# One kilobyte-sized load, two queues: the convolution taps issued by ScalarE instead of SyncE

## The chip, the core and the metric

The kernel runs on one core of a Trainium2 chip. The core has five engines with an instruction queue each: TensorE (PE, matmuls and their weight loads PEld), VectorE (DVE), ScalarE (ACT), GpSimd (POOL) and SyncE (SP, which only issues transfers here). Engines work through their own instructions in order and wait for each other by semaphores. Sixteen DMA engines move data. A queue name with a q at the end (SPq, ACTq, PEq) is an engine's instruction queue: what it shows is issue or waiting, not computing.

The metric is the device time in microseconds (us) of one execution. Before the change it is 263.19 us, the median of three runs (262.81 to 263.39).

## What is computed

One layer of a model on 2048 tokens of width 640: a LayerNorm, a gated long convolution (A), and a gated feed-forward block with 1728 inner columns (B), both with a residual sum. Cut to what matters:

```python
def A(q, k, v, shift_k, ssm_k, ssm_D):           # q is LayerNorm(x)
    k_shift = sum(k_pad[:, t:t+S, :] * shift_k[:, 3-t] for t in range(4))   # 4 taps per channel
    kv = k_shift * v
    y = irfft(rfft(kv, 2*S) * rfft(ssm_k, 2*S))[:S]                         # causal convolution of length S
    return q * (y + kv * ssm_D)

def B(x, w_gate, w_up, w_down):
    return (silu(x @ w_gate) * (x @ w_up)) @ w_down

x = A_q
h  = x + A(layernorm(x), A_k, A_v, A_shift_k, A_ssm_k, A_ssm_D)
h2 = h + B(layernorm(h), B_w_gate, B_w_up, B_w_down)
```

`A_shift_k`, the taps, is a 640 x 4 array in bf16, 5 KB in all.

## The kernel before

The 2048 tokens are cut into four blocks of 512. A block's 512 tokens lie as 128 partitions times four rows. For each block the kernel forms kv (shift convolution of k, times v), transforms kv and the long filter with matrices of cosines and sines held in `WF`, multiplies and sums the spectra on VectorE, transforms back with `WI`, and runs LayerNorm and the feed-forward block. All phases of all blocks are interleaved.

The interleaving is written out by hand. The kernel first makes a list of operations (`plan.add`, with the helpers `pe`, `act`, `dve`, `load`, `evict`), numbered in the order in which the code adds them. `Plan.run` (L147) then goes through the tuple `ORDER` (L43) and emits the operations in that order; a negative entry ~n means operation n with its other engine (a PSUM copy on VectorE instead of ScalarE). Each operation's instructions go to their engine's queue in the order of emission. So the table sets the order within every engine, and the waits between engines follow from who reads and writes what. On-chip buffers come from small pools (four PSUM buffers `ps`, twelve `big`, five `row` and so on) and are handed out in table order, the oldest free one first.

The beginning of the table, which is what the change touches:

```python
ORDER = (
    0, 3, 1, 18, 19, 20, 21, 26, 5, 4, 11, 12, 9, 7, 8, 22, 23, 10, 24, -26, 27, 28, 29, ...
    ... 14, 13, 191, 16, 17, 15, 193, 350, ... 418, 6, 32, 30, 31, 33, 34, 37, 35,
    -37, 38, 41, -43, 118, 39, 40, 65, -67, ... 56, ...
```

The operations with their lines in the profile:

- 0 and 1 (L866, L867): the identity matrix for transposes, made by VectorE and GpSimd.
- 3 and 4 (L471, SyncE): the two halves of block 0 of k. 11, 12, 14 and 13 (L276, L271, L264, L900, SyncE): block 0 of q (`x`), of v and of the filter `ssm_k` (`g`), and `WF`.
- **5 (L875, SyncE): the taps.** The 640 x 4 array is read as five partitions of 1 KB, into the tile `tap5` (`tap` in the profile).
- 18 to 25: the four rows of k are transposed by PE (L484, five matmuls of 128 x 128 each) and copied from PSUM (L486): 19, 21 and 23 by ScalarE, 25 (entry -26) by VectorE.
- 7 (L886): PE turns the taps with four small transposes. 8 (L888): ScalarE copies them to `tapw`. 9 (L892, L893) folds the identity into a small one, and 10 (L895, VectorE) makes `diag`, the taps on small diagonals.
- 27 and 32 (L505): the shift convolution as matmuls of k against `diag`, 112 for four groups of 128 channels, 28 for the fifth. 28 to 31, 33 and 34 (L527, VectorE): the products with v.
- 6 (L880): 24 matmuls of the identity with itself, whose result nobody reads. They keep PE at work between 27 and 32.
- 35 to 42: g is transposed by PE (L392) and copied (L394), rows 0 and 3 by VectorE and 1 and 2 by ScalarE.
- 110 to 117: the first LayerNorm's statistics, two sweeps over each of the four rows of q by ScalarE (L630 the means, L578 the squares).
- 65, 56 and so on (L309): the forward transforms of kv and g, copied from PSUM at L298 (ScalarE) and L301 (VectorE).

In each engine's own queue the start thus reads as follows.

- SyncE: 3, 5, 4, 11, 12, 14, 13, then the transposing loads of the next block of k (L473).
- PE: 18, 20, 7, 22, 24, 27, 6, 32, 37, 35, 41, 39, 65, 56.
- ScalarE: a table load, 19, 21, 8, 23, the eight statistics, 38, 40.
- VectorE: 0, 26, 9, 10, 25, 28 to 31, 33, 34, 36, 42.

Of the kernel before, what the change touches and what calls it, by code (L numbers as in the profile page):

```python
# [19 lines left out]
P = 128  # L20
# [151 lines left out]
def kernel(ctx: ExitStack, tc: tile.TileContext, A_q, A_k, A_v, A_shift_k, A_ssm_k, A_ssm_D, B_x,  # L172
          B_w_gate, B_w_up, B_w_down, out):
    nc = tc.nc
# [20 lines left out]
    def new(kind):  # L195
        return Buf(views.get(kind, (kind,))[0], kind)

    def fixed(shp, dt, name):
        return Buf(None, None, const.tile(shp, dt, name=name))

    def ap(b):
        if b.pool is None:
            return b.ap
        t = place[b.pool][b.at]
        _, how, sizes = views.get(b.kind, (None, None, None))
        return t.rearrange(how, **sizes) if how else t
# [15 lines left out]
    def load(nbytes, fn, w, r=()):  # L222
        return plan.add("sp", nbytes / 300.0, fn, r, w)
# [27 lines left out]
    tap5 = fixed([KT, P * 4], BF16, "tap5")  # L251
# [214 lines left out]
    def load_k(j):  # L466

        kT = new("kT")
        if j == 0 and not K0TURN:
            for lo in (0, 2):  # L470
                load(MB // 2, lambda lo=lo: nc.sync.dma_start(out=plain(kT)[:, lo:lo + 2], in_=block(kk, j)[:, lo:lo + 2, :]), [(kT, ("in", lo // 2))])  # L471
        for r in range(R) if j or K0TURN else ():
            plan.add("turn", MB / 4 / 300.0, lambda r=r: nc.sync.dma_start(  # L473
                out=ap(kT)[:, :, r, PAD:], in_=block(kk, j)[:, r, :], transpose=True), [], [(kT, r)])
        return kT
# [396 lines left out]
            nc.gpsimd.memset(t[64:P, NC_FULL, :], 0.0)  # L872
    plan.add("pool", 2000, blank, [], [blanks])
    k = load_k(0)
    load(1e3, lambda: nc.sync.dma_start(out=ap(tap5), in_=A_shift_k.rearrange("(c p) t -> c (p t)", p=P)), [tap5])  # L875
    idle = new("ps")

    def warm():
# [43 lines left out]
    for j in range(1, NB):  # L922
        plan.block = j
        g = load_g(j)
        if j == 1:
            load(P * NC_FULL * D * 2, lambda: nc.sync.dma_start(
                out=ap(wd)[:, 0:NC_FULL, :], in_=B_w_down[0:NC_FULL * P, :].rearrange("(c p) d -> p c d", p=P)), [(wd, 0)])
# [67 lines left out]
```

## Time and profile before

| | |
|---|---|
| median of three runs | 263.19 us (262.81 to 263.39) |
| the profiled execution's own time | 263.05 us |
| its span, first to last instruction | 261.4 us |
| PE busy in the span | 249.5 us, 95% |
| VectorE busy | 207.8 us, 79% |
| ScalarE busy | 172.9 us, 66% |
| mean granted TensorE clock | 0.999 |
| moved by DMA | 40.82 MB, mean 156 GB/s |

Times in the views are counted from the start of the span. A row of the chain of waits reads: start, length, what. A row of the timeline reads: start, length, engine, line, operation, output <- input, shape, count of merged instructions, and in brackets how long the engine had been idle and what ended it. "x10" rows merge ten instructions; the length is that of the whole row. Matmuls are pipelined, so that the length of one matmul is longer than the distance between two. The landing time of a transfer is counted from its issue.

### The profile page before, as it was taken

Reading aid. Unit: us, or ns where it says so; the run is one execution under the profiler, and the core shown is the slowest. Engines: PE = TensorE matmul, PEld = TensorE weight load, DVE = VectorE, ACT = ScalarE, POOL = GpSimd, SP = SyncE. Lnnn points to the kernel's source line nnn. Section 1 sums busy time; section 2 is a strip of 40 time slices with the busy share of each in tenths; the row PEclk is TensorE's granted clock in tenths of the full one; section 3 lists DMA queues with packets and bytes.
Section 4 is the critical chain, followed back from the end, with each engine's and each line's share of the span. In section 5 each row is a group of like instructions: output and inputs, shape, how many; then the busy total and the mean of one; then the engine's idle time right before and its main releaser. Section 6 shows DMA issues by size and latency. Waiting matters only on the chain.

```text
span 261.4 us, 5121 instructions
## 1 busy us (share of the span) xinstructions
PE 249.5 (95%) x2040; PEld 148.1 (57%) x2040; DVE 207.8 (79%) x325; ACT 172.9 (66%) x294; POOL 18.3 (7%) x26
## 2 busy tenths in 40 slices
PE   3989997999999999999999999999999999999995
PEld 2866674544555677654446667544447764444673
DVE  1579999999999999999999999999999831122132
ACT  4798999999959788757787857154465744434300
POOL 0001000001200013000001300200040121000000
PEclk9999999999999999999999999999999999999999
DMA  6999698998887669579077606796299942000002
GB/s 199 301 235 265 179 174 181 278 261 179 249 277 209 148 127 204 119 223 271 19 212 116 101 0 73 185 286 162 52 319 246 218 50 25 3 0 0 0 15 87
DMA packets 73235, 40.82 MB, mean 156 GB/s; under 512 B 33462, under 2 KB 71164, under 8 KB 73212
## 3 DMA queue, kind: packets, MB, share of 16 engines
q1 hardware_dynamic: 70908, 37.88, 58.2%
q0 software_dynamic: 2304, 2.62, 7.0%
q8 instruction: 16, 0.26, 0.4%
q14 instruction: 7, 0.06, 0.1%
HBM read 30.01 MB, written 4.59 MB: 132 GB/s over the span
## 4 chain that ended last, share of the span: by engine, by line
PE 72%; DVE 14%; ACT 7%; DMA 3%; issue 2%; SPq 0%; ACTq 0%
PE ps L776 32%; PE ps L843 22%; PE ps L309 9%; PE ps L696 4%; PE ps L811 4%; DMA big<-in_A_q_dram 3%; DVE S L539 2%; ACT S L298 2%; DVE S L566 2%; DVE big L565 2%; ACT row L578 2%; DVE big L539 2%; DVE tT L802 1%; ACT row L630 1%; DVE S L437 1%
## 5 line engine op out<-in xcount | busy, mean ns | idle before, releaser
L776 PE MATMUL ps<-big,big 128*128 128x512 bf16 x480 | 105.8, 379 | 0.3 <-ACT sg L820 0.2
L776 PEld LDWEIGHTS <-big 128*128 128x128 bf16 x480 | 46.8, 98 | 56.1 <-issue 1.1
L843 PE MATMUL ps<-wd,tT 128*128 128x320 bf16 x448 | 63.5, 299 | 0.0
L843 PEld LDWEIGHTS <-tT 128*128 128x128 bf16 x448 | 43.7, 98 | 17.4
L793 ACT ACTIVATE sg<-ps 128x1024 bf16<-128x1024 f32 (+1 forms) x28 | 27.0, 965 | 34.7 <-PE ps L776 17.6
L309 PE MATMUL ps<-big,WF 128*128 128x320 bf16 x224 | 35.6, 299 | 1.9 <-ACT big L394 0.8
L566 DVE TENSOR_TENSOR S<-S,big 128x2560 bf16<-128x2560 bf16 x24 | 35.2, 1479 | 0.0
L565 DVE TENSOR_TENSOR big<-S,S 128x2560 bf16<-128x2560 bf16 x24 | 35.2, 1479 | 0.0
L802 DVE TENSOR_TENSOR tT<-sg,sg 128x1024 bf16<-128x1024 bf16 (+1 forms) x26 | 16.7, 642 | 19.4 <-ACT sg L800 19.3
L309 PEld LDWEIGHTS <-WF 128*128 128x128 bf16 x224 | 21.8, 97 | 13.2 <-issue 3.3
L800 ACT CAST sg<-ps 128x1024 bf16<-128x1024 f32 (+1 forms) x26 | 24.6, 947 | 4.9 <-PE ps L776 4.8
L578 ACT ACTIVATE row<-big 128x640 bf16<-128x640 bf16 x32 | 23.6, 742 | 3.7 <-DVE big L714 3.3
L298 ACT CAST S<-ps 128x320 bf16<-128x320 f32 (+1 forms) x36 | 18.0, 547 | 3.8 <-PE ps L309 3.4
L641 ACT ACTIVATE row<-big,sm 128x640 bf16<-128x640 bf16 x18 | 15.8, 916 | 6.0 <-DVE sm L591 6.0
L849 POOL DMA_DIRECT2D out_dram<-row x12 | 10.6, 1022 | 96.5 <-ACT row L848 95.0
L696 PEld LDWEIGHTS <-WI 128*128 128x128 bf16 x128 | 12.4, 98 | 6.0 <-issue 1.1
L696 PE MATMUL ps<-S,WI 128*128 128x320 bf16 x96 | 15.0, 299 | 0.4 <-DVE S L539 0.4
L298 ACT ACTIVATE big<-ps 128x640 bf16<-128x640 f32 (+1 forms) x23 | 13.9, 634 | 2.1 <-PE ps L309 2.0
L811 PE MATMUL ps<-big,big 128*128 128x512 bf16 x60 | 14.3, 379 | 0.0
L708 DVE SCALAR_TENSOR_TENSOR row<-row,ps 128x640 bf16<-128x640 bf16 x16 | 12.8, 813 | 0.2
L630 ACT ACTIVATE row<-big 128x640 bf16<-128x640 bf16 x16 | 11.8, 740 | 1.6 <-DMA big<-in_A_q_dram 1.6
L539 DVE TENSOR_TENSOR big<-S,S 128x2560 bf16<-128x2560 bf16 (+1 forms) x10 | 12.1, 1219 | 0.1
(83 smaller groups left out, 229.2 us busy)
## 6 DMA issues: line engine op xcount, KB each, us to landing
big<-in_B_w_up_dram SPq DMA_DIRECT2D x24, 320.0 KB, 5.1
big<-in_B_w_gate_dram SPq DMA_DIRECT2D x24, 320.0 KB, 5.0
big<-in_A_q_dram SPq DMA_DIRECT2D x4, 640.0 KB, 4.7
big<-in_A_v_dram SPq DMA_DIRECT2D x4, 640.0 KB, 4.3
big<-in_A_ssm_k_dram SPq DMA_DIRECT2D x4, 640.0 KB, 8.2
wd<-in_B_w_down_dram SPq DMA_DIRECT2D x1, 2080.0 KB
out_dram<-big SPq DMA_DIRECT2D x3, 640.0 KB, 5.3
out_dram<-row POOLq DMA_DIRECT2D x12, 160.0 KB, 5.4
```

Source lines behind the costliest of these rows:

```text
L298: (lambda: nc.scalar.activation(dst(), src(), ACT.Copy, scale=2.0)) if twice else (lambda: nc.scalar.copy(dst(), src())),
L309: nc.tensor.matmul(ap(ps)[:, h, 0:NH], w, ap(src)[:, r, h * NH:(h + 1) * NH], start=(first and i == 0), stop=(last and i == len(rs) - 1), ...
L539: return lambda: f(*(x() for x in args))
L565: dve(1490, lambda b=b, xs=xs, hs=hs: nc.vector.tensor_mul(flat2(b), X.part(xs), H.part(hs)), [X.at(xs), H.at(hs)], [b])
L566: dve(1490, lambda b=b, dst=dst, f=f: f(A.part(dst), A.part(dst), flat2(b)), [b], [A.at(dst)])
L578: act(930, lambda r=r, junk=junk: nc.scalar.activation(ap(junk), ap(x)[:, r, :], ACT.Square, scale=D ** -0.5, accum_out=sm(s, 1)[:, r:r + ...
L696: nc.tensor.matmul(ap(ps)[:, w, 0:NH], m, src[:, w * NH:(w + 1) * NH], start=(i == 0), stop=(i == len(terms) - 1))
L776: nc.tensor.matmul(of(ps, i), ap(w)[:, k, off:off + P], ap(hT)[:, k, lo:lo + n], start=(k == 0), stop=(k == KT - 1))
L793: act(1010 if wide else 600, lambda: nc.scalar.activation(of(sg), of(*gate), ACT.Silu), [gate[0]] if gate[0] is up[0] else [(gate[0], gate ...
L800: op = plan.add("act", 1010 if wide else 590, lambda: nc.scalar.copy(of(co), of(*up)), psu + [sg], [co] + tt, ("dve", 1230 if wide else 69 ...
L811: nc.tensor.matmul(ap(ps)[:, i, :], ap(w)[:, k, off:off + P], ap(hT)[:, k, :], start=(k == 0), stop=(k == KT - 1))
L843: nc.tensor.matmul(ap(to)[:, hf, 0:NH], ap(tT)[:, c, at:at + P], ap(wd)[:, c, hf * NH:(hf + 1) * NH], start=(c == order[0]), stop=(c == or ...
```

## The change

One word changes: the load of the taps is started on ScalarE's queue instead of SyncE's.

```diff
     k = load_k(0)
-    load(1e3, lambda: nc.sync.dma_start(out=ap(tap5), in_=A_shift_k.rearrange("(c p) t -> c (p t)", p=P)), [tap5])
+    load(1e3, lambda: nc.scalar.dma_start(out=ap(tap5), in_=A_shift_k.rearrange("(c p) t -> c (p t)", p=P)), [tap5])
     idle = new("ps")
```

The list of operations, their numbers and the order table stay as they are, and operation 5 keeps its place in the table: behind 21 and 26, ahead of 4. SyncE's queue has one issue less, ScalarE's one more. The other transfers stay on SyncE.

## The prediction

> **What bounds the kernel now.** I read the chain of work that ended last first, because a start-up load matters only if the chain passes through it.
>
> ```profile
> 1.28 0.35 SPq L875
> 1.63 0.05 issue
> 1.68 0.35 SPq L471
> ...
> 2.08 6.85 DMA big<-in_A_q_dram
> ...
> 8.95 0.83 ACT row L630 x2
> ...
> 14.82 0.58 ACT big L394
> ...
> 15.45 7.77 PE ps L309 x54
> ```
>
> Columns: start, length, what. The chain begins in SyncE's issues, the taps (L875) among them, goes through the landing of q at 8.93, then through ScalarE's eight LayerNorm statistics (L630, L578) to the copy at L394, which gives back a PSUM buffer; only then does PE begin the long run of transform matmuls at 15.45. So the first 15.45 us are ScalarE's, and ScalarE's start is the landing of q. The next question is whether a shift at 15.45 is swallowed later. The table of stretches (busy PE, PEld, DVE, ACT, POOL in turn) answers it:
>
> ```profile
> 15.45:26.50 11.05, 11.05 (x78) 7.42 (x77) 9.12 (x21) 9.92 (x28) 0.70 (x1) 1.00 1.16 249
> 26.50:54.00 27.50, 25.44 (x299) 16.15 (x299) 26.26 (x55) 27.25 (x46) 0.00 (x0) 1.00 0.91 199
> 54.00:88.00 34.00, 33.66 (x312) 17.84 (x311) 34.00 (x41) 30.20 (x54) 2.75 (x3) 1.00 0.89 240
> 88.00:261.40 173.40, 169.61 (x1145) 98.49 (x1144) 131.74 (x194) 95.67 (x147) 14.11 (x16) 1.00 0.52 118
> ```
>
> In each stretch one engine has almost no idle time: PE 11.05 of 11.05, ACT 27.25 of 27.50, DVE 34.00 of 34.00, PE 169.61 of 173.40. There is no slack in which a late start disappears, so I carry a shift at 15.45 to the end one for one.
>
> The start itself, in order of time (start, length, engine, line, work, and in brackets the idle time before it and what ended it):
>
> ```profile
> 4.07 1.25 PE L484 MATMUL ps<-ident,kT 128*128 128x128 bf16 x10 [4.07 <-DMA kT<-in_A_k_dram]
> 4.82 1.29 ACT L486 COPY kT<-ps 128x640 bf16<-128x640 bf16 x2 [2.72 <-PE ps L484]
> ...
> 5.25 0.29 PE L886 MATMUL ps<-ident,tap 5*128 5x5 bf16 x4
> ...
> 5.94 1.25 PE L484 MATMUL ps<-ident,kT 128*128 128x128 bf16 x10 [0.40 <-DMA kT<-in_A_k_dram]
> 5.99 0.23 ACT L888 COPY tapw<-ps 128x20 bf16<-128x20 bf16 x1
> 6.26 0.82 DVE L895 TENSOR_TENSOR diag<-eye,tapw 128x640 bf16<-128x640 bf16 x1 [4.38 <-ACT tapw L888]
> 6.70 0.69 ACT L486 COPY kT<-ps 128x640 bf16<-128x640 bf16 x1 [0.47 <-PE ps L484]
> ...
> 7.14 2.30 PE L505 MATMUL ps<-diag,kT 32*128 32x128 bf16 x112
> ...
> 8.95 0.74 ACT L630 ACTIVATE row<-big 128x640 bf16<-128x640 bf16 x1 [1.57 <-DMA big<-in_A_q_dram]
> ...
> 9.37 2.54 PE L880 MATMUL ps<-ident 128*128 128x128 bf16 x24
> ...
> 10.60 3.15 DVE L527 TENSOR_TENSOR big<-ps,big 128x512 bf16<-128x512 f32 x6 [2.88 <-DMA big<-in_A_v_dram]
> ...
> 12.39 0.47 PE L392 MATMUL ps<-ident,big 128*128 128x128 bf16 x5
> ...
> 13.13 1.11 PE L392 MATMUL ps<-ident,big 128*128 128x128 bf16 x15 [0.28 <-DVE big L527]
> ...
> 14.19 0.43 PE L309 MATMUL ps<-big,WF 128*128 128x320 bf16 x2
> ...
> 14.72 1.26 ACT L394 COPY big<-ps 128x640 bf16<-128x640 bf16 x2
> ...
> 15.45 4.41 PE L309 MATMUL ps<-big,WF 128*128 128x320 bf16 x30 [0.82 <-ACT big L394]
> ```
>
> The taps' four small transposes (L886) ran at 5.25 straight behind the first ten transposes of k: the taps had landed by then and nobody waited. Behind them on PE stand the other ten transposes of k, the shift convolution (L505), the block of 24 filler matmuls (L880) and the transposes of g (L392), all in order. PE reaches 14.62 (14.19 + 0.43) and then waits until 15.45 for ScalarE. PE has 0.83 us to spare at that point, ScalarE none.
>
> **The change, part by part.**
>
> *What SyncE saves.* One issue of 0.35 and a gap of 0.05: the second half of k, q, v, ssm_k and WF are issued 0.40 us earlier. That is the gross gain, and it stands on the chain. But the DMA engines are already full:
>
> ```profile
> 2.00:2.50 0.50, 0.00 (x0) 0.00 (x0) 0.00 (x0) 0.10 (x1) 0.00 (x0) 1.00 0.92 164
> ...
> 8.00:9.00 1.00, 1.00 (x80) 1.00 (x71) 0.00 (x0) 0.05 (x1) 0.12 (x1) 1.00 0.94 290
> ```
>
> The last two numbers are the DMA engines' busy share and GB/s: 0.92 from 2.0 us on and 0.94 when q lands. A load that queues behind others lands when the bytes ahead of it are through, whatever its issue time. So q gains something between 0 and 0.40 us; I take 0.1.
>
> *What ScalarE gets, and where.*
>
> ```profile
> 2.08 0.43 SPq L276 DMA_DIRECT2D big<-in_A_q_dram  x1
> ...
> 3.50 0.52 SPq L900 DMA_DIRECT2D WF<-const_wf  x1
> ```
>
> SyncE's issues come in the table's order (k, taps, k, q, v, ssm_k, WF are operations 3, 5, 4, 11, 12, 14, 13: L471, L875 and L471 in the chain above, and q first and WF last in this timeline), so I take each engine to follow the table. There operation 5 stands behind 19 and 21, ScalarE's first two copies of transposed k (L486), and these wait for PE. The issue can't go out before the second copy has been handed on. When is that?
>
> ```profile
> 5.41 0.70 ACT L486 COPY kT<-ps 128x640 bf16<-128x640 bf16 x1
> ```
>
> ```profile
> L394 ACTq EVENT_SEMAPHORE  x1: 17/17/17, 13.8 to 13.8; - x1
> ```
>
> The second copy starts at 5.41 and ends at 6.11. The second row shows ScalarE's queue passing a wait of L394 at 13.8, while the copy itself starts at 14.72: the queue runs ahead of the engine. So the taps are issued at 5.41 at the earliest and 6.11 at the latest, against 1.28 now; I take 5.41. The issue costs ScalarE's queue 0.35 by SyncE's row, and that lies under the running copy.
>
> *How long the transfer takes.* No DMA on ScalarE's queue is in this trace, so I bound it by its neighbours (sizes, then median us from issue to landing):
>
> ```profile
> kT<-in_A_k_dram SPq DMA_DIRECT2D x2, 320.0 KB, 4.2
> ...
> WF<-const_wf SPq DMA_DIRECT2D x1, 512.0 KB, 10.2
> ...
> out_dram<-row SPq DMA_DIRECT2D x2, 80.0 KB, 1.6
> wd<-in_B_w_down_dram SPq DMA_DIRECT2D x1, 80.0 KB, 2.4
> ```
>
> From below 1.6, the quickest row, a store at the end with nothing beside it; from above 4.2, half of k in this very stretch with sixty times the bytes. The taps are a small load among full DMA engines, nearest to the 80 KB load with 2.4; for the traffic I take 2.6. So the taps land at T = 5.41 + 2.6 = 8.0, with bounds of 7.0 (5.41 + 1.6) and 10.3 (6.11 + 4.2), instead of by 5.25.
>
> Here the Trainium skill (DMA: Bandwidth & Descriptors, section "Issuing engines are not separate DMA queues") speaks against the move: transfers started by different engines run on the same 16 DMA engines and interleave, and a second issuer saves only sequencer time, usually small beside the transfer. By it the gain is at most the 0.40 of issue time, and the taps get no faster path; the sum stays as it is. The 0.94 busy share above agrees.
>
> *What is queued behind the late taps: PE.* L886 starts at T and takes 0.29; the ten transposes of k behind it, whose data came by 5.94, led to L505 in 7.14 − 5.94 = 1.20, so L505 starts at T + 1.49. The other way to L505 gives the same: 0.29, a hand-over of about 0.1, the copy 0.23, diag 0.82 and two small gaps, T + 1.5. With T = 8.0 that is 9.5 instead of 7.14, 2.36 later. L505, L880 and the first L392 follow without waits of note, so the first L392 is at 12.39 + 2.36 = 14.75. The products on DVE (L527), which waited for v until 10.60, now wait for L505 (9.44 + 2.36 + 0.1 = 11.9), 1.3 later; that is less than PE's shift, so PE's stall of 0.28 goes. With it and a little of the gap at g's landing gone, L392 ends about 2.0 later, 14.24 → 16.2. The two first L309 (0.43) make it 16.6, against 15.45 now: **+1.1** by PE, or T − 6.9 in general.
>
> *What is queued behind them: ScalarE.* The copy at L888 waits for L886, and the third copy of k (L486) for the later transposes: before, it began 6.70 − 5.94 = 0.76 behind their start, now at T + 0.29 + 0.76 = T + 1.05, and ends at T + 1.74 = 9.74. The statistics can't begin before that; they began at 8.95. So +0.8 there, and L394 and the buffer it frees move from 15.45 to 16.25: T − 7.2 in general. ScalarE's idle 1.57 before q covers the rest of the delay; without that cover it would be 2.4.
>
> *The sum.* PE and ScalarE must both arrive, so the later counts: +1.1 at 15.45 (PE), and then one for one. The 0.1 that q gains is on ScalarE's path, which no longer decides. The profiled execution took 263.05 us (span 261.4 and 1.65 around it), the median of the runs shown is 263.19, 0.14 more, which is inside their spread. 263.05 + 1.1 = **264.15 us**. With T from 7.0 to 10.3 the shift goes from 0.1 to 3.4.
>
> **The rivals.**
>
> *The taps come early enough and q's earlier issue counts (the other side).* If T is below 6.5, PE's T − 6.9 is −0.4 and ScalarE's T + 1.74 is before the landing of q, so the chain starts up to 0.40 earlier: 262.65. That takes a landing 1.1 us after 5.41, quicker than any row (1.6), or an issue ahead of the copies, which SyncE's obedience to the table speaks against; and q has to follow its issue although the DMA engines are full.
>
> *The cover just holds.* With T near 7.0 (a transfer of 1.6, as the end stores show) the shift is 0.1: 263.1, no change that can be told.
>
> *The taps wait behind everything queued.* At 5.41, q, v, ssm_k and WF are under way. If a transfer comes only after them, T is 8.95 behind q alone, or 3.50 + 10.2 = 13.7 behind WF (issue row plus its landing row): shifts of 2.05 and 6.8, so 265.1 to 269.85. For it: the engines' 0.94. Against it: the taps stand in a queue of their own. The same page, section "Queues, rings and completion order", says that a DMA engine takes turns between the queues that have work, a packet at a time; by that rule the far end is excluded. No run yet shows it here.
>
> *PE's clock comes late.* The matmul's length shows the clock:
>
> ```profile
> L880 PE MATMUL ps<-ident x24: 219/311/312, 9.4 to 11.7; 128*128 128x128 bf16 x24
> ```
>
> ```profile
> L392 PE MATMUL ps<-ident,big x20: 216/218/246, 12.4 to 14.0; 128*128 128x128 bf16 x20
> ```
>
> Minimum, median and maximum ns: most of the filler block ran at 311, its last ones and L392 at 218. The full rate came near 11.4, some 4.3 us behind the start of L505. PE now idles from 5.3 to T. I have the rate come 4.3 behind the new L505, at 13.8, in time for L392. If it comes after L392, its 20 matmuls take 0.106 (2.54 / 24) instead of about 0.064 ((1.11 − 0.22) / 14) each, 0.84 more: 265.0. If it comes at 11.4 as before, the filler block shrinks by about 1.0, PE falls behind ScalarE, and ScalarE's +0.8 decides: 263.85. The Trainium skill (TensorE: Matmul & The Clock Gate, Part 1) says that full rate follows a busy window of about 3.4 us and that the windows run free of the kernel, so the instant may vary from run to run; it favours neither.
>
> **How the numbers follow.** Forecast (T from 7.5 to 9, +0.6 to +2.1) 0.50; clock late 0.10; behind the queue 0.12; cover holds 0.16; early and faster 0.12. Time: 264.15. The range reaches down into the cases without loss and up to T = 9.8 (+2.9): 262.8 to 266.0, leaving out the far end of the queue case, the upper bound of the transfer, and the best of the faster one. A difference of 0.2% (0.53 us) is about what a measurement of this kernel can tell from none; so slower is 0.50 + 0.10 + 0.12 = 0.72, same 0.16, faster 0.12.
>
> **What would show it.** An L875 row on ACTq between 5.4 and 6.1; L886 at 7 to 10 with an idle time of 2 or more ended by the DMA of the taps; L505 1.5 behind it; L630 at about 9.7, released by L486 and not by q; the second run of L309 near 16.5; and the rest of the chain with the same length as before. Wrong I am if the issue stands ahead of the copies, if L886 starts before 7, or if the shift at L309 is not found again in the span.

## The result, and the profile after

The changed kernel takes 265.83 us (median of six runs, 265.17 to 266.69), the kernel before 262.84 (six runs beside it, 261.79 to 263.39). The ratio is 1.0118 with a 95% interval of 1.0089 to 1.0146: some 3 us slower, well clear of no change. A second series gave 266.12 against 262.89, ratio 1.0126 (1.0087 to 1.0165). The prediction was 264.15 with a range of 262.8 to 266.0. The direction was right, the loss of 1.1 was a good third of what came. The time lies 0.17 inside the upper end of the range; the second series lies 0.12 beyond it.

The timeline of the start of the changed kernel, in the form shown before:

```profile
3.67 1.25 PE L484 MATMUL ps<-ident,kT 128*128 128x128 bf16 x10 [3.67 <-DMA kT<-in_A_k_dram]
4.42 0.69 ACT L486 COPY kT<-ps 128x640 bf16<-128x640 bf16 x1 [2.32 <-PE ps L484]
4.96 0.55 ACTq L875 DMA_DIRECT2D tap<-in_A_shift_k_dram  x1
5.01 0.70 ACT L486 COPY kT<-ps 128x640 bf16<-128x640 bf16 x1
...
9.41 0.29 PE L886 MATMUL ps<-ident,tap 5*128 5x5 bf16 x4 [4.49 <-DMA tap<-in_A_shift_k_dram]
...
9.63 1.25 PE L484 MATMUL ps<-ident,kT 128*128 128x128 bf16 x10
...
10.38 0.69 ACT L486 COPY kT<-ps 128x640 bf16<-128x640 bf16 x1 [0.43 <-PE ps L484]
...
10.86 2.26 PE L505 MATMUL ps<-diag,kT 32*128 32x128 bf16 x112
...
10.97 0.74 ACT L630 ACTIVATE row<-big 128x640 bf16<-128x640 bf16 x1
...
13.05 2.74 PE L880 MATMUL ps<-ident 128*128 128x128 bf16 x24
...
16.12 1.37 PE L392 MATMUL ps<-ident,big 128*128 128x128 bf16 x20
...
16.73 1.49 ACT L394 COPY big<-ps 128x640 bf16<-128x640 bf16 x2
...
17.45 2.61 PE L309 MATMUL ps<-big,WF 128*128 128x320 bf16 x18
```

The issue of the taps (L875) starts on ScalarE's queue at 4.96, beside the second copy of k at 5.01. The taps' transposes (L886) wait for the transfer until 9.41; PE is idle for 4.49 us. ScalarE's first statistic (L630) starts at 10.97 with no wait for q. q had landed at 8.3, and ScalarE was busy with the copy of k right ahead of it, whose row runs to 11.07 (neighbouring rows overlap by 0.1).

How much of this reaches the end? The chain of waits of this kernel doesn't answer, because it can be followed back only to 138 us. The same instruction in both kernels does. VectorE's first long subtraction (L344) and one of its sums 80 us later (L539) in the kernel before:

```profile
20.37 0.82 DVE L344 TENSOR_TENSOR S<-big,S 128x1280 bf16<-128x1280 bf16 x1
```

```profile
100.03 1.49 DVE L539 TENSOR_TENSOR S<-S,big 128x2560 bf16<-128x2560 bf16 x1
```

and in the changed kernel:

```profile
22.61 0.81 DVE L344 TENSOR_TENSOR S<-big,S 128x1280 bf16<-128x1280 bf16 x1
```

```profile
102.29 1.49 DVE L539 TENSOR_TENSOR S<-S,big 128x2560 bf16<-128x2560 bf16 x1
```

The start is 2.24 us late (22.61 − 20.37) and nothing of it is regained in 80 us (102.29 − 100.03 = 2.26). The whole span grew by 3.1 (261.4 to 264.5). Most of the rest comes at one place, a wait of VectorE for a store at L638; first the kernel before, then the changed one:

```profile
103.94 0.45 DVE L638 TENSOR_SCALAR row<-big,sm 128x640 bf16<-128x640 bf16 x1 [0.17 <-DMA out_dram<-row]
```

```profile
107.22 0.45 DVE L638 TENSOR_SCALAR row<-big,sm 128x640 bf16<-128x640 bf16 x1 [1.18 <-DMA out_dram<-row]
```

0.17 us became 1.18, which is 1.0 of the 3.1. Whether this second loss belongs to the change is one question for the experiments; the other is why a transfer of 5 KB took 4.4 us.

### The profile page after: what moved, and what is told of

Read it like the earlier page. It is cut to its first block, busy times and chain, and to the rows that moved or that the text cites. A ratio compares the mean times of both kernels' runs of the same rounds, so it can differ in the third digit from the quotient of the medians.

```text
span 264.5 us, 5121 instructions
## 1 busy us (share of the span) xinstructions
PE 249.5 (94%) x2040; PEld 148.0 (56%) x2040; DVE 207.9 (79%) x325; ACT 173.0 (65%) x294; POOL 17.2 (7%) x26
## 5 line engine op out<-in xcount | busy, mean ns | idle before, releaser
L578 ACT ACTIVATE row<-big 128x640 bf16<-128x640 bf16 x32 | 23.6, 742 | 3.9 <-DVE big L714 3.5
L696 PEld LDWEIGHTS <-WI 128*128 128x128 bf16 x128 | 12.3, 98 | 6.8 <-issue 1.3
L539 DVE TENSOR_TENSOR big<-S,S 128x2560 bf16<-128x2560 bf16 (+1 forms) x10 | 12.1, 1220 | 0.1
L539 DVE TENSOR_TENSOR S<-S,big 128x2560 bf16<-128x2560 bf16 (+1 forms) x10 | 12.1, 1218 | 0.0
```

Of the source, the lines that this page charges most:

```text
L539: return lambda: f(*(x() for x in args))
L578: act(930, lambda r=r, junk=junk: nc.scalar.activation(ap(junk), ap(x)[:, r, :], ACT.Square, scale=D ** -0.5, accum_out=sm(s, 1)[:, r:r + ...
L696: nc.tensor.matmul(ap(ps)[:, w, 0:NH], m, src[:, w * NH:(w + 1) * NH], start=(i == 0), stop=(i == len(terms) - 1))
```

## The experiments

Experiments change the place of operations in the order table and nothing else, but for the one that says otherwise. Medians are set against the kernel before in the same series. "Issue to L886" is the time from the start of the taps' issue to the start of their transposes.

### The changed kernel again

> The changed kernel once more, to see what repeats. Theory 'late taps, one for one': the taps (issued at about 5.0) land again near 9.4 and L886 starts there; the copies at L298 and all that follows are 2.2 us later at 20 us; the total is 2.2 us above the kernel before plus whatever VectorE's wait for a store at L638 adds near 105 us (it was 0.17 us long before and 1.18 after). Rival 'the second loss belongs to the change': that wait is 1.2 us long again, total +3.1 to +3.3. If the wait differs from one profile to the next (between 0 and 1.2), it is not the change's.

Measured: 266.12 against 262.89, ratio 1.0126 (1.0087 to 1.0165). Its timeline, at the taps and at VectorE's L344:

```profile
5.20 0.56 ACTq L875 DMA_DIRECT2D tap<-in_A_shift_k_dram  x1
...
10.29 0.29 PE L886 MATMUL ps<-ident,tap 5*128 5x5 bf16 x4 [5.13 <-DMA tap<-in_A_shift_k_dram]
```

```profile
23.27 0.81 DVE L344 TENSOR_TENSOR S<-big,S 128x1280 bf16<-128x1280 bf16 x1
```

The taps came 0.9 later still, 5.1 us from the issue, and L344 is 2.90 late. The waits of this execution between 95 and 116 us show none of VectorE at L638. The total rose all the same: this very execution took 265.82, 2.93 above the median before. So the wait at L638 isn't what makes the changed kernel slow.

### The taps first on ScalarE's queue

```diff
-    0, 3, 1, 18, 19, 20, 21, 26, 5, 4, 11, 12, 9, 7, 8, 22, 23, 10, 24, -26, 27, 28, 29, 225, 113, 117, 111, 116,
+    0, 3, 5, 1, 18, 19, 20, 21, 26, 4, 11, 12, 9, 7, 8, 22, 23, 10, 24, -26, 27, 28, 29, 225, 113, 117, 111, 116,
```

> The same ScalarE queue, but operation 5 stands at the front of the table, behind operation 3, so ScalarE issues the taps at about 0.8, ahead of its table load and of the copies. Theory 'place': only the place behind the copies cost time. L886 then runs at about 4.9 behind the first transposes of k with no wait for the taps, q lands 0 to 0.4 earlier than before because SyncE is still relieved of its issue, and the total is 0 to 0.4 us under the kernel before (ratio 0.9985 to 1.000). Rival 'queue': a transfer on ScalarE's queue is slow wherever it stands (4.4 us from issue to landing, as in the changed kernel); L886 then waits until 5.2 or later, and the total is no better than before.

> The kernel with the taps first on ScalarE's queue once more, because its profile had its start 0.60 us earlier and its median only 0.07 lower. Theory 'the gain is there': L309 again at 14.8 to 15.1 in the profile, ratio 0.997 to 0.999. Rival 'it drowns': ratio 0.999 to 1.001, whatever the one profile shows.

Measured: 262.82 against 262.89, ratio 1.000 (0.9976 to 1.0024), and in the second series 263.12 against 263.21, ratio 0.9994 (0.9968 to 1.0019). The second profile's start:

```profile
3.74 1.25 PE L484 MATMUL ps<-ident,kT 128*128 128x128 bf16 x10 [3.74 <-DMA kT<-in_A_k_dram]
...
4.92 0.29 PE L886 MATMUL ps<-ident,tap 5*128 5x5 bf16 x4
5.15 1.25 PE L484 MATMUL ps<-ident,kT 128*128 128x128 bf16 x10
...
8.12 0.74 ACT L630 ACTIVATE row<-big 128x640 bf16<-128x640 bf16 x1 [1.53 <-DMA big<-in_A_q_dram]
...
14.62 4.41 PE L309 MATMUL ps<-big,WF 128*128 128x320 bf16 x30 [0.76 <-ACT big L394]
```

On the same queue, issued at 0.82 ahead of everything, the taps are there when PE gets to them: the whole loss is gone. It is the place, not the queue as such. SyncE's relief shows too: q lands at 8.1 and the start is 0.83 earlier than in the first profile of the kernel before (14.62 against 15.45; the first of the two had 14.85). In the medians it is 0.07 and 0.09. "It drowns" held for the medians; the second interval still allows anything from a gain of 0.8 to a loss of 0.5 us.

### The kernel before again

> The kernel before, for a second profile of the same start. Theory: q lands at 8.9 again and the second run of L309 starts at 15.4 again, so the 8.0 to 8.6 of the kernels that issue q 0.34 us earlier is a true gain of 0.3 to 0.9. Rival: the landing of q scatters by half a microsecond from one execution to the next, and the first profile was a late one; then q lands below 8.6 here too.

One execution, 265.72 us, more than any of the 17 runs beside it (261.83 to 264.79). Its start:

```profile
9.31 0.74 ACT L630 ACTIVATE row<-big 128x640 bf16<-128x640 bf16 x1 [2.04 <-DMA big<-in_A_q_dram]
...
14.25 1.89 PE L392 MATMUL ps<-ident,big 128*128 128x128 bf16 x20 [1.46 <-DMA big<-in_A_ssm_k_dram]
```

```profile
DVE row L638 <- DMA out_dram<-row: 1.2, 1, 1.2
```

```profile
22.21 0.82 DVE L344 TENSOR_TENSOR S<-big,S 128x1280 bf16<-128x1280 bf16 x1
```

q landed at 9.3, and ssm_k at 14.2 instead of 12.3, so PE waited 1.46 us for it. Between these two executions of the unchanged kernel the landing of q differs by 0.4 us and that of ssm_k by 1.9; one profile can't price an issue of 0.40. L344 starts at 22.21 here, 1.84 later than in the first profile, with the taps in time. So a start shift read from a single pair of profiles, such as the 2.24, carries this scatter too; that the change costs 3 us rests on the medians. The row of L638 is a sum of waits (waiting for what, us, times, longest): the store at L638 held VectorE for 1.2 us here, without the change. So that wait belongs to neither kernel: it was 0.17 and 1.2 in the two executions of the kernel before, 1.18 and none in the changed kernel's, none and 0.8 with the taps first on ScalarE's queue.

### Late taps without ScalarE's queue

The kernel before, with SyncE issuing the taps behind q, or behind q and v:

```diff
-    0, 3, 1, 18, 19, 20, 21, 26, 5, 4, 11, 12, 9, 7, 8, 22, 23, 10, 24, -26, 27, 28, 29, 225, 113, 117, 111, 116,
+    0, 3, 1, 18, 19, 20, 21, 26, 4, 11, 5, 12, 9, 7, 8, 22, 23, 10, 24, -26, 27, 28, 29, 225, 113, 117, 111, 116,
```

```diff
-    0, 3, 1, 18, 19, 20, 21, 26, 5, 4, 11, 12, 9, 7, 8, 22, 23, 10, 24, -26, 27, 28, 29, 225, 113, 117, 111, 116,
+    0, 3, 1, 18, 19, 20, 21, 26, 4, 11, 12, 5, 9, 7, 8, 22, 23, 10, 24, -26, 27, 28, 29, 225, 113, 117, 111, 116,
```

> The taps back on SyncE, but issued behind q (operations 3, 4, 11, 5, 12). A late landing without ScalarE's queue. If transfers of one queue go through in the order of issue, the taps land with q, at 8.3 to 8.9; by the rule of the sum (start shift T - 6.9, one for one) the start shifts by 1.4 to 2.0 and the total by as much, 264.2 to 264.9. Rival 'it is ScalarE's issue that costs': no loss beyond 0.3 us, because ScalarE issues nothing here.

> As the run before, but the taps behind v too (3, 4, 11, 12, 5). A second dose: with v the taps land at 9.8 to 10.5, so start shift and total are +2.9 to +3.6 us. Rival: if small transfers overtake big ones of their own queue, T stays under 8 in both runs and the loss under 1.1.

Measured: behind q 263.49 against 262.89, ratio 1.0015 (0.9989 to 1.0041); behind v 267.01, ratio 1.0146 (1.0111 to 1.0181). Behind q, then behind v:

```profile
8.28 0.29 PE L886 MATMUL ps<-ident,tap 5*128 5x5 bf16 x4 [3.34 <-DMA tap<-in_A_shift_k_dram]
```

```profile
10.45 0.29 PE L886 MATMUL ps<-ident,tap 5*128 5x5 bf16 x4 [5.49 <-DMA tap<-in_A_shift_k_dram]
```

On one queue the taps land with the load ahead of them (q at 8.3, v at 10.2). The changed kernel's 9.4 and 10.3 are the landing of a load behind v. And lateness alone makes the loss, with no issue on ScalarE: L344 started 1.19 late behind q (21.56) and 3.06 late behind v (23.43). The total behind q rose by 0.6, less than the 1.19 of its one profile and below the 264.2 to 264.9 that were expected; the interval reaches from −0.3 to +1.1, so the one-for-one rule is neither shown nor refuted by this run. Behind v it rose by 4.1 (2.9 to 4.8) for a start 3.06 late.

### What the taps wait for

The changed kernel, with loads moved behind the first transposing load of k's next block (operation 191), which SyncE can't issue before the taps have been used. WF moved; ssm_k too; v too; q too:

```diff
-    114, 110, 112, 115, 14, 13, 191, 16, 17, 15, 193, 350, 187, 192, 190, 194, 418, 6, 32, 30, 31, 33, 34, 37, 35,
+    114, 110, 112, 115, 14, 191, 13, 16, 17, 15, 193, 350, 187, 192, 190, 194, 418, 6, 32, 30, 31, 33, 34, 37, 35,
```

```diff
-    114, 110, 112, 115, 14, 13, 191, 16, 17, 15, 193, 350, 187, 192, 190, 194, 418, 6, 32, 30, 31, 33, 34, 37, 35,
+    114, 110, 112, 115, 191, 14, 13, 16, 17, 15, 193, 350, 187, 192, 190, 194, 418, 6, 32, 30, 31, 33, 34, 37, 35,
```

```diff
-    0, 3, 1, 18, 19, 20, 21, 26, 5, 4, 11, 12, 9, 7, 8, 22, 23, 10, 24, -26, 27, 28, 29, 225, 113, 117, 111, 116,
-    114, 110, 112, 115, 14, 13, 191, 16, 17, 15, 193, 350, 187, 192, 190, 194, 418, 6, 32, 30, 31, 33, 34, 37, 35,
+    0, 3, 1, 18, 19, 20, 21, 26, 5, 4, 11, 9, 7, 8, 22, 23, 10, 24, -26, 191, 12, 27, 28, 29, 225, 113, 117, 111, 116,
+    114, 110, 112, 115, 14, 13, 16, 17, 15, 193, 350, 187, 192, 190, 194, 418, 6, 32, 30, 31, 33, 34, 37, 35,
```

```diff
-    0, 3, 1, 18, 19, 20, 21, 26, 5, 4, 11, 12, 9, 7, 8, 22, 23, 10, 24, -26, 27, 28, 29, 225, 113, 117, 111, 116,
-    114, 110, 112, 115, 14, 13, 191, 16, 17, 15, 193, 350, 187, 192, 190, 194, 418, 6, 32, 30, 31, 33, 34, 37, 35,
+    0, 3, 1, 18, 19, 20, 21, 26, 5, 4, 9, 7, 8, 22, 23, 10, 24, -26, 191, 11, 12, 27, 28, 29, 225, 113, 117, 111, 116,
+    114, 110, 112, 115, 14, 13, 16, 17, 15, 193, 350, 187, 192, 190, 194, 418, 6, 32, 30, 31, 33, 34, 37, 35,
```

> The changed kernel with SyncE's load of WF moved behind the first transposing load of k's next block, so that WF (512 KB) is not issued when ScalarE issues the taps. What does the landing of the taps wait for? Theory 'turn in the DMA engines': the taps wait for packets that stand ahead of them, of k, q and v; WF's packets come behind them anyway (they began at 9.0), so the taps land near 9.4 as before. Rival 'making the descriptors': ScalarE's request waits until SyncE's earlier requests, WF last, have been turned into descriptors; without WF the taps land 0.5 us earlier or more, at 8.9 or below. WF itself lands late and the total is not to be read.

> The changed kernel with ssm_k and WF moved behind the transposing load of k's next block; q and v stay where they are. Until now: issue to landing 4.4 to 5.1 us with all four loads under way, 4.5 with WF gone, 1.6 with all four gone. Theory 'the taps wait for what the DMA engines have taken in ahead of them, v and a part of ssm_k': without ssm_k the wait ends when v is through on most engines (near 7.6 in the changed kernel), so the taps land at 7.7 to 8.5. Rival 'a fixed wait, long whenever the engines are busy': 9.4 or later as before. Second rival 'only q and k count': v makes no difference either, landing at 6.5 to 7.0. ssm_k and WF come late, so the total is not to be read.

> The changed kernel with only q in front: v, ssm_k and WF come behind the transposing load of k's next block. So far the taps on ScalarE's queue landed within 0.6 us of v (9.4 to 10.3 against 9.6 to 10.2) whether or not ssm_k and WF were under way, and 1.6 us after the issue when q and v were gone too. Theory 'the taps come after the bytes that were handed to the DMA engines before them': with only q in front they land near q, at 7.5 to 8.5, or earlier if the engines are through with q sooner. Rival 'a fixed wait beside any traffic': 9.4 or later again. Rival 'only v matters': 6.6 to 7.0. v and the rest come late, so the total is not to be read.

> The changed kernel with q, v, ssm_k and WF all moved behind that transposing load, so that at the taps' issue only the two halves of k are under way. Theory 'waiting behind other loads': issued at about 5.0, the taps land within 1.6 to 2.4 us, at 6.6 to 7.4. Rival 'ScalarE's queue is slow by itself': they land 4.4 us after the issue as in the changed kernel, at 9.4. The loads come late here, so the total is some us above the changed kernel and says nothing on the taps.

The totals (266.21, 268.32, 268.22 and 268.76 in one run each) carry the late loads and aren't read. The timelines at L875 and L886, in the same order:

```profile
5.29 0.56 ACTq L875 DMA_DIRECT2D tap<-in_A_shift_k_dram  x1
...
9.84 0.29 PE L886 MATMUL ps<-ident,tap 5*128 5x5 bf16 x4 [4.59 <-DMA tap<-in_A_shift_k_dram]
```

```profile
5.00 0.55 ACTq L875 DMA_DIRECT2D tap<-in_A_shift_k_dram  x1
...
10.10 0.29 PE L886 MATMUL ps<-ident,tap 5*128 5x5 bf16 x4 [5.15 <-DMA tap<-in_A_shift_k_dram]
```

```profile
5.18 0.55 ACTq L875 DMA_DIRECT2D tap<-in_A_shift_k_dram  x1
...
7.61 0.29 PE L886 MATMUL ps<-ident,tap 5*128 5x5 bf16 x4 [2.47 <-DMA tap<-in_A_shift_k_dram]
```

```profile
5.23 0.55 ACTq L875 DMA_DIRECT2D tap<-in_A_shift_k_dram  x1
...
6.85 0.29 PE L886 MATMUL ps<-ident,tap 5*128 5x5 bf16 x4 [1.66 <-DMA tap<-in_A_shift_k_dram]
```

Landings of v and q are their issue plus their landing rows:

| under way beside k | issue to L886 | L886 | landing of the last of q and v |
|---|---|---|---|
| q, v, ssm_k, WF (changed kernel) | 4.45 | 9.41 | v 9.9 |
| the same, again | 5.09 | 10.29 | v 9.6 |
| q, v, ssm_k | 4.55 | 9.84 | v 10.0 |
| q, v | 5.10 | 10.10 | v 10.2 |
| q | 2.43 | 7.61 | q 7.4 |
| nothing | 1.62 | 6.85 | |

Taking away WF and ssm_k brings nothing, so the rival that the request waits for WF to be made into descriptors is not borne out. Taking away v brings 2.7 us; q brings another 0.8, little more than the 0.6 by which the two profiles of the changed kernel differ. Each row is one execution. Alone, the transfer takes 1.6 us, the lower bound of the prediction. So ScalarE's own queue gave most of the taps no way past q and v. My guess for the second of these runs (ssm_k moved too), that the wait would end when v is through on most engines (7.7 to 8.5), was wrong: it ended near v's last landing (10.10 against 10.2). The trace's packets of the taps show the same: a packet takes 0.046 us, but in the changed kernel the first of the five starts at 8.57, 3.6 us behind the issue, against 6.16, 0.93 behind it, with nothing in front.

The packets also show how far the other loads had got, since the loads differ in packet size. When the first packet of the taps started in the changed kernel, 244 of the 256 packets of q and v had started, and 324 of the 640 of ssm_k. In its repeat all 256 had started, and 449 of ssm_k; in both, none of WF. So the taps didn't come straight behind v: where ssm_k was under way, half of its packets or more went first, too. With only q in front, three of their five packets started before q's last.

### Fewer filler matmuls

```diff
-WARM = 24
+WARM = 6
```

> The changed kernel with 6 filler matmuls (L880) instead of 24; their result is read by nobody. Theory 'PE decides the start': in the changed kernel the filler block of 2.74 us is on the late path, ScalarE's path is only 0.2 us behind PE's. Cutting 18 of 24 brings PE's transposes of g some 1.9 us forward, ScalarE then decides (16.73 at L394), and the start shift falls from 2.24 to about 2.0 us; the total gains about 0.2 us on the changed kernel. Rival 'PE alone decides': the total gains 1.5 us or more. Second rival 'PE's clock': without the block the transforms run at half rate at first, and the total loses.

Measured: 265.85 against 262.81, ratio 1.0115 (1.0085 to 1.0144); the taps landed at 9.9.

```profile
17.20 0.43 PE L309 MATMUL ps<-big,WF 128*128 128x320 bf16 x2
17.23 1.26 ACT L394 COPY big<-ps 128x640 bf16<-128x640 bf16 x2
17.95 3.33 PE L309 MATMUL ps<-big,WF 128*128 128x320 bf16 x22 [0.33 <-ACT big L394]
```

18 matmuls less on PE's late path brought nothing that can be told: PE is now early and waits 0.33 for ScalarE. "PE alone decides", by which 1.5 us or more would have been gained, is refuted. A loss through the clock doesn't show: 3.0 us above the kernel before, as with the whole block. With taps this late, ScalarE sets the start nearly by itself.

## Why the prediction was right or wrong

**Place of the issue: right.** It was foreseen at the second copy of k; it stands at 4.96 beside a copy at 5.01 (5.20 and 5.25 the second time). It is earlier than 5.41 because k landed earlier. It takes 0.55 instead of 0.35 and is hidden under the copy, as foreseen.

**Time of the transfer: the step that failed.** "For the traffic I take 2.6. So the taps land at T = 5.41 + 2.6 = 8.0". Issue to L886 was 4.45 and 5.09, beyond the upper bound of 4.2, and T 9.41 and 10.29. The neighbours were chosen by size, while what counted is the loads handed over before: alone the taps take 1.6, behind q 2.4, behind q and v 4.4 to 5.1. That the total still lay inside the range is in part luck: its upper end stood for T = 9.8, between the two T that were measured. The upper bound came from a load with nothing but another half of k before it. The right row stood in the same profile: v, issued at 2.55, landed 8.0 later.

**The rival of the queue: right in kind.** It named q (T = 8.95) and WF (13.7) as the loads to wait for; it was q, v and, by the packets, half of ssm_k or more. The page of the Trainium skill cited there (DMA: Bandwidth & Descriptors, section "Queues, rings and completion order") lets a DMA engine take turns between queues packet by packet. Here the trace agrees in that the taps didn't wait for all that was issued before them: their first packet started ahead of every packet of WF. It doesn't show whether turns were taken; if they were, one lasted long, for the taps waited 2.8 to 3.5 us beyond the 1.6 alone. The chance of 0.12 was too small.

**Behind the taps.** L505 came 1.45 behind L886 (10.86 − 9.41), foreseen 1.49. ScalarE's start of the statistics came 1.56 behind it, foreseen 1.74. With the T that was measured, its rule, shift = T − 7.2, gives 2.2, 3.1, 1.1 and 3.25 for the changed kernel, its repeat and the two kernels with late taps on SyncE; L344 shows 2.24, 2.90, 1.19 and 3.06. PE's rule, T − 6.9, gives 0.2 to 0.5 too much: the forecast took the larger of the two and so the one that fits less well, which is small beside the error in T. PE's clock is part of it: in the changed kernel all 24 filler matmuls took 2.74 us, in its repeat 1.83, so the full rate came at different instants, as that rival allowed, and PE made up what it was behind.

**One for one: held over 80 us** (2.24 to 2.26). What came on top in one profile, the wait at L638, came in the unchanged kernel as well. Start shifts of 2.24 and 2.90 stand beside 3.0 and 3.2 in the medians; the difference is below what the intervals (2.3 to 3.8 and 2.3 to 4.3 us) tell apart.

**What SyncE saves.** Predicted 0.1 of 0.40 for q. In nine executions with the earlier issue and v behind q as usual q landed at 7.9 to 8.6, against 8.9 and 9.3 in two without. So in the profiles it is 0.3 to 1.4, more than 0.1, though the two without differ by 0.4 between themselves; but with ScalarE behind the taps nobody waits for q, and where somebody does (taps first), the medians show 0.07 and 0.09. The rival "early and faster" had its condition met by that kernel; its 0.40 doesn't show in the medians, but lies within the intervals.

## What to carry to other kernels

A transfer issued from another engine starts where that engine's own order lets it, so the place in the order table matters more than the queue; here the front of ScalarE's order costs nothing that can be told and the place behind two copies 3 us. A small load that was issued behind big ones here came when they did, on either queue: with q ahead of it at 7.6 and 8.3, with v too at 9.41 to 10.45. So price such a load by the landing of the loads ahead of it, not by its size. Where the landings of the first loads scatter by 0.4 to 1.9 us, a gain of 0.4 us of issue time was not to be told from none.

## What was not expected of the hardware

Two queues meant little overtaking: 5 KB on ScalarE's queue landed within 0.7 us of 640 KB of v on SyncE's queue, which had been issued 2.8 us earlier, in the midst of ssm_k's packets, issued 2.3 us earlier, and ahead of the landing of ssm_k and of WF, issued 1.8 us earlier. Why the line falls there was not tried: whether the DMA engines took turns, or had taken in that much before the taps came, stays open. An issue costs 0.55 to 0.56 us on ScalarE's queue and 0.35 to 0.37 on SyncE's, for the same transfer.
